# Counting four token tiles per matmul in the routing rounds with 32 thresholds

## The chip, the cores and the metric

The program runs on one core of one Trainium2 chip. The metric is device time in microseconds (us) of one execution. The engines of the core work in parallel, each through its own queue of instructions in order: PE (TensorE, matmuls; its weight loads are shown as PEld), DVE (VectorE), ACT (ScalarE), POOL (GpSimd) and SP (SyncE, which here issues DMAs).

## What is computed

Three blocks stand behind one another: a linear attention over 8 batches, 8 heads, 576 tokens and 64 channels; a mixture of experts with exact, balanced routing; a feed-forward block of width 2048. The change lies in the routing of the second:

```python
N, D = x.shape                  # 4608, 512
E = w_gate.shape[1]             # 8 experts
cap = N // E                    # 576 tokens for each
flat = (x @ w_gate).flatten()
for idx in np.argsort(-flat):
    tok, e = (int(idx) // E, int(idx) % E)
    if assigned[tok] >= 0 or counts[e] >= cap:
        continue
    assigned[tok] = e
    counts[e] += 1
...
out[mask] = np.maximum(x[mask] @ w1[e], 0.0) @ w2[e]
```

So the token-expert pairs are taken from the largest logit down, and an expert that has its 576 tokens is closed.

## The kernel before, in words

**The routing** goes in 8 phases, `route(ph)` for `ph` 0 to 7. Each phase finds the expert that fills up next and the list of its 576 tokens. It looks at every token's best logit among the experts still open and searches the value at which the first expert has 576 tokens above it. The search reads the logit as a number of 31 bits and settles some bits at a time in six rounds; `ROUNDS` (line 539) gives shift and number of thresholds: two rounds with 64 thresholds, then four with 32. The last phase needs no search, so seven phases have rounds: 42 in all, 28 of them with 32 thresholds.

The 4608 tokens lie as 36 tiles (`NJ`) of 128 partitions. One round (`round`, lines 845 to 899) is a chain that goes to and fro between DVE and PE:

- `cmp` (line 860, DVE) compares every token with all thresholds: `cm`, 128 partitions by 36 tiles by thresholds, ones and zeros in bf16.
- `count` (line 872, PE) multiplies `cm` (stationary operand) with `C` (moving operand, 8 columns for each tile, a one at the token's best expert) and sums over tiles in a PSUM bank `c4`. It steps by two tiles: 18 products, each with 16 moving columns (the experts of tiles j and j+1). With 32 thresholds the stationary operand is four tiles wide all the same, 128 columns; the rows of the third and fourth tile are computed and not used. The last step (j = 34) has only two tiles left, 64 columns; it is put ahead of j = 32, so that the sum's last product is again 128 wide.
- `flags` (lines 877 and 878, DVE): of `c4` only two blocks mean something, rows of the first tile against its experts and rows of the second against its own. One instruction takes the second block negated into `odd`, one compares first block minus 576 with `odd`.
- `bcast` (line 883, PE) and `accum` (lines 887 and 890, DVE) turn the flags into the settled digit and the tokens' next digits, from which the next round's `cmp` starts.

After the rounds the phase picks the expert, ranks its tokens and makes the list `ix` (line 818), which gates the gathers of that expert's tokens (`xg`, line 956, POOL queue) and of its weights (`wst`, line 928, POOL queue).

**What runs beside it.** Phase 0 runs while attention ends. Phases 1 to 7 run inside the expert stage: for each expert, 16 steps of 12 matmuls into `hp` (line 998) and, two steps later, 12 into `yp` (line 1017); ACT and DVE make `hh` from `hp` in two parts (lines 1005 and 1009). DVE and ACT also split each expert's gathered weights into two halves (`unit`, lines 909 and 915), transpose results into `xT` (lines 973 and 977, after PE's transposes `tp`, line 967), and convert the weights of the third block (`convert_w`, lines 1099 to 1204), which SP stores to DRAM (`wdi`, line 1215) and loads again (line 1271). The units are 24 buffers that expert weights, converted weights and loads share.

**What sets the order.** A planner (`Sched`, lines 45 to 149) writes the whole stage out by hand: every step is entered with an engine, an assumed cost, what it reads and writes and a priority, and the planner issues, again and again, the step that could start first by these costs. The order on every queue comes from this plan; on the chip each engine takes its queue in order. Expert products are taken in their sequence and have the routing ahead of them (`p = -1000 + 26.51 * ph`, line 636). One plan covers the routing's phases 1 to 7 and nearly the whole expert stage; attention with phase 0 has a plan before it, and the end of the last expert and the third block have plans after it.

Of the kernel before, what the change touches and what calls it, by code (L numbers as in the profile page):

```python
# [14 lines left out]
OP = mybir.AluOpType  # L15
# [6 lines left out]
E, F, FF = 8, 1024, 2048  # L22
CAP = NT // E
NJ = NT // 128
# [587 lines left out]
class Moe:  # L612
# [17 lines left out]
    def route(self, ph, bank):  # L630
# [7 lines left out]
        def dve(cost, fn, r=(), w=(), early=False, slack=0.0):  # L638
            sc.op("DVE", cost, fn, r=[(x, ph) if isinstance(x, str) else x for x in r],
                  w=[(x, ph) if isinstance(x, str) else x for x in w], prio=0 if early else p, slack=slack, port=early)  # L640

        def pe(cost, fn, r=(), w=(), new=()):
            sc.op("PE", cost, fn, r=[(x, ph) for x in r], w=[(x, ph) for x in w], prio=p,
                  new=[("rt" if ph else "mT", (x, ph)) for x in new], slack=SLACK if ph else 0.0)
# [127 lines left out]
        def onehot(g0, g1):  # L772
            if g0 == 0:
                T["A"] = sm.tile([128, NG, 64, 2], BF, name="A", tag="cm")
            sh = [128, g1 - g0, 64, 2]
            V.tensor_tensor(T["A"][:, g0:g1], two(T["qr"][:, 0])[:, g0:g1, None, :].to_broadcast(sh),
                            c["i64"][:, None, :, :].to_broadcast(sh), op=OP.is_equal)
# [9 lines left out]
        dve(0.9, pay, r=["qr"], w=["P"])  # L787
        CH = [(0, 9), (9, 18)] if ph == 0 else [(0, 18)]
        for g0, g1 in CH:
            dve(0.0 + 0.0705 * (g1 - g0), lambda g0=g0, g1=g1: onehot(g0, g1), r=["qr"], w=["A%d" % g0] + (["A"] if g0 == 0 else []))  # L790

        def lists(g0, g1):
            if g0 == 0:
                T["ls"] = bank()
            for g in range(g0, g1):
                nc.tensor.matmul(T["ls"][:, 0:4 * NQ], T["A"][:, g].rearrange("p r j -> p (r j)"),
                                 T["P"][:, g].rearrange("p a q j -> p (a q j)"),
                                 start=(g == 0), stop=(g == NG - 1))
        for g0, g1 in CH:
            pe(0.027 * (g1 - g0), lambda g0=g0, g1=g1: lists(g0, g1), r=["A", "A%d" % g0, "P"], w=["ls"],  # L800
# [44 lines left out]
    def round(self, ph, T, n, dve, pe, bank, cuts, allw, allv):  # L845
        nc, c, sm = self.nc, self.c, self.sm
        V = nc.vector
        sh, NT_ = ROUNDS[n]
        lone = len(cuts) > 2
        first = lone and n == 0  # L850
        CH = list(zip(cuts, cuts[1:])) if first else ((0, 24), (24, NJ)) if lone and NT_ > 32 else ((0, NJ),)

        def cmp(j0, j1):
            if j0 == 0:
                T["cm"] = sm.tile([128, NJ // 2, 64, 2], BF, name="cm").rearrange("p g t j -> p (g t j)")[:, 0:NJ * NT_].rearrange(
                    "p (j t) -> p j t", t=NT_)
            if n == 0:
                T["x"] = T["x0"]
            s = [128, j1 - j0, NT_ // 2, 2]
            V.tensor_tensor(T["cm"][:, j0:j1].rearrange("p j (h i) -> p j h i", i=2), T["x"][:, j0:j1, None, :].to_broadcast(s),  # L860
                            c[f"tab{n}"].rearrange("p (h i) -> p h i", i=2)[:, None, :, :].to_broadcast(s), op=OP.is_ge)

        def count(j0, j1):

            if j0 == 0:
                T["c4"] = bank()
            js = list(range(j0, j1, 2))
            if NT_ < 64:
                js[-2:] = js[:-3:-1]
            for j in js:  # L870
                w = min(128 // NT_, j1 - j)
                nc.tensor.matmul(T["c4"][0:w * NT_, 0:2 * E], T["cm"][:, j:j + w].rearrange("p j t -> p (j t)"),  # L872
                                 self.C[:, j:j + 2].rearrange("p j e -> p (j e)"), start=(j == 0), stop=(j1 == NJ and j == js[-1]))

        def flags():
            odd = sm.tile([64, E], F32, name="odd")[0:NT_]
            V.tensor_scalar(odd, T["c4"][NT_:2 * NT_, E:2 * E], -1.0, None, op0=OP.mult)
            V.scalar_tensor_tensor(self.flags[NT_][0:NT_], T["c4"][0:NT_, 0:E], float(CAP), odd, op0=OP.subtract, op1=OP.is_ge)

        def bcast():  # L880
            t = T["nb"] = bank()
            T["nb"] = t[:, 0:E]
            nc.tensor.matmul(t[:, 0:E], c["step"][:, n:n + 1].to_broadcast([128, 128]), self.flags[NT_], start=True, stop=True)

        def accum():
            ns = T["ns"] = sm.tile([128, 1], F32, name="ns", bufs=4)
            V.tensor_reduce(ns, T["nb"], axis=AX, op=OP.max)
            if n + 1 < NR:
                x = sm.tile([128, NJ, 2], BF, name="x", bufs=2)
                V.scalar_tensor_tensor(x, T["x"], ns, T["w"][:, n + 1, :, None].to_broadcast([128, NJ, 2]), op0=OP.subtract, op1=OP.add)  # L890
                T["x"] = x
        c4, nb, fl = f"c4{n}", f"nb{n}", f"fl{n}"
        for j0, j1 in CH:
            dve(0.07 + 0.00052 * NT_ * (j1 - j0), lambda j0=j0, j1=j1: cmp(j0, j1), r=["w%d" % j0, "cm"][:2 if j0 else 1] if first else allw + ["cm"] * (j0 > 0) + ["acc"] * (n > 0) + [("ls", ph - 1)] * (n == 0 and ph > 0),
                w=["cm%d" % j0] + ["cm"] * (j0 == 0), early=first and j1 < NJ)
            pe(0.0135 * (j1 - j0), lambda j0=j0, j1=j1: count(j0, j1), r=["cm%d" % j0] + allv, w=[c4], new=[c4] if j0 == 0 else [])
        dve(0.28, flags, r=[c4], w=[fl])
        pe(0.06, bcast, r=[fl], w=[nb], new=[nb])
        dve(0.4 if n + 1 < NR else 0.1, accum, r=[nb] + allw, w=["acc"])

# [756 lines left out]
```

## Time and profile before

| what | value |
|---|---|
| time, median of 3 runs (lowest, highest) | 1421.38 us (1420.37, 1422.38) |
| the profiled execution's own time | 1418.27 us |
| its span, first to last instruction | 1416.5 us |
| mean granted TensorE clock over the span | 0.983 of full speed |
| attention and routing phase 0 | about 0 to 178 us |
| expert stage with routing phases 1 to 7 | about 178 to 645 us |
| feed-forward block | about 645 to 1416 us |

The profile shows one execution. Busy times are per engine, idle time stands in brackets with what ended it, and a matmul's length holds its run through the array: matmuls overlap, so what a group of them takes of PE is read from its start to the start of what comes next.

### The profile page before, as it was taken

What the parts mean: (1) busy time and instruction counts of PE and PEld (TensorE: products, weight loads), DVE (VectorE), ACT (ScalarE), POOL (GpSimd) and SP (SyncE); (2) the same over time, 40 slices, a digit from 0 to 9 for tenths busy, and PEclk for the clock granted to TensorE, in tenths of its full rate; (3) what the DMA queues carried; (4) which work ended last, traced back from release to release, by engine and by line L of the source; (5) the groups of instructions that cost most, each with busy time, mean ns of one, the idle gap of its engine ahead of it and who ended that gap; (6) DMA issues with size and microseconds to landing.
All of it is one profiled execution on the core that took longest, in us unless ns stands there. A gap on an engine that the chain in (4) does not pass through costs nothing.

```text
span 1416.5 us, 26771 instructions
## 1 busy us (share of the span) xinstructions
PE 1336.9 (94%) x10256; PEld 1236.3 (87%) x10256; DVE 1047.9 (74%) x2207; ACT 789.9 (56%) x1513; POOL 275.8 (19%) x314
## 2 busy tenths in 40 slices
PE   4888399999999999998999999999999999999997
PEld 4777299989999899998998989989899999999996
DVE  7797778889878767736777776877767676776664
ACT  4675125334434545535766765767667676675663
POOL 8897322332223121000001010100101000010101
PEclk9999599999999999999999999999999999999999
DMA  9997424535745979757966575766667556765640
GB/s 264 258 265 284 129 83 143 172 118 181 221 126 167 321 231 319 206 186 270 348 207 195 179 231 171 231 208 186 202 199 248 171 188 194 229 206 172 201 164 30
DMA packets 161919, 286.98 MB, mean 203 GB/s; under 512 B 25600, under 2 KB 101376, under 8 KB 161792
## 3 DMA queue, kind: packets, MB, share of 16 engines
q1 hardware_dynamic: 137680, 222.35, 51.5%
q0 software_dynamic: 15040, 52.44, 11.3%
q10 hardware_dynamic: 9072, 10.49, 2.1%
q8 instruction: 81, 1.33, 0.4%
q14 instruction: 46, 0.38, 0.1%
HBM read 235.95 MB, written 49.28 MB: 201 GB/s over the span
## 4 chain that ended last, share of the span: by engine, by line
PE 56%; issue 28%; DMA 5%; DVE 4%; POOL 3%; SPq 2%; ACT 2%; ACTq 0%; POOLq 0%; DVEq 0%
PE hp L998 14%; PE yp L1017 13%; PE yp L1483 12%; PE hp L1357 11%; PE rt L872 2%; POOL out_dram L1495 2%; DMA kh<-in_k_dram 1%; DMA wdi<-unit 1%; PE tp L967 1%; DMA q<-in_q_dram 1%; PE xp L433 1%; SPq L212 1%; DMA xg<-xd,ix 1%; DMA v<-in_v_dram 1%; DVE cm L860 0%
## 5 line engine op out<-in xcount | busy, mean ns | idle before, releaser
L1483 PE MATMUL yp<-unit,g 128*128 128x512 f32 x1728 | 431.4, 392 | 0.1
L1483 PEld LDWEIGHTS yp<-unit,g 128*128 128x128 f32 x1728 | 310.0, 188 | 56.2 <-DVE g L1395 1.0
L1357 PEld LDWEIGHTS hp<-yTa,unit 128*128 128x128 f32 x2256 | 288.4, 188 | 18.5 <-DVE hp L1446 2.9
L1357 PE MATMUL hp<-yTa,unit 128*128 128x256 f32 x2256 | 294.1, 280 | 4.1 <-DVE hp L1446 2.7
L998 PE MATMUL hp<-xT,unit 128*128 128x288 f32 x1536 | 283.0, 303 | 0.2 <-DVE hh L1009 0.2
L1017 PE MATMUL yp<-hh,unit 128*128 128x288 f32 x1500 | 265.7, 297 | 0.0
L998 PEld LDWEIGHTS hp<-xT,unit 128*128 128x128 f32 x1536 | 228.5, 190 | 1.0 <-DVE hh L1009 0.4
L1017 PEld LDWEIGHTS yp<-hh,unit 128*128 128x128 f32 x1500 | 221.1, 189 | 0.3 <-ACT ys L1024 0.2
L1495 POOL DMA_INDIRECT out_dram<-os,gix x36 | 38.1, 1059 | 799.6 <-ACT os L1491 455.1
L1005 ACT ACTIVATE hh<-hp 128x288 fp32r<-128x288 f32 x125 | 51.2, 409 | 216.0 <-PE hp L998 191.0
L1365 ACT ACTIVATE u<-hp 128x512 f32<-128x512 f32 x144 | 86.0, 597 | 117.7 <-PE hp L1357 112.3
L1382 DVE SCALAR_TENSOR_TENSOR u<-w,r 128x512 f32<-128x512 f32 x144 | 98.7, 687 | 45.4 <-ACT r L1379 44.8
L1392 ACT ACTIVATE g<-w 128x512 fp32r<-128x512 f32 x144 | 90.3, 628 | 74.5 <-DVE w L1388 73.6
L928 POOL DMA_INDIRECT wst<-in_moe_w_dram,wi x64 | 67.1, 1048 | 246.7 <-DVE unit L915 62.3
L1009 DVE SCALAR_TENSOR_TENSOR hh<-hp,hh 128x288 fp32r<-128x288 f32 x125 | 57.0, 456 | 76.4 <-ACT hh L1005 75.7
L909 ACT ACTIVATE unit<-wst 128x512 fp32r<-128x512 f32 x128 | 77.9, 646 | 48.4 <-DMA wst<-in_moe_w_dram,wi 30.5
L1395 DVE TENSOR_TENSOR g<-w,g 128x512 fp32r<-128x512 f32 x144 | 98.8, 686 | 5.6 <-ACT g L1392 4.1
L1388 DVE SCALAR_TENSOR_TENSOR w<-r,hp 128x512 f32<-128x512 f32 x144 | 98.3, 684 | 5.5
L1357 PEld LDWEIGHTS hp<-yTb,unit 128*128 128x128 f32 x768 | 99.2, 191 | 3.6
L1357 PE MATMUL hp<-yTb,unit 128*128 128x256 f32 x768 | 102.1, 283 | 0.0
L1385 DVE SCALAR_TENSOR_TENSOR r<-u,r 128x512 f32<-128x512 f32 x144 | 98.8, 687 | 1.9
L1368 DVE TENSOR_SCALAR u<-u 128x512 f32<-128x512 f32 x144 | 61.0, 425 | 50.9 <-ACT u L1365 50.4
(205 smaller groups left out, 1711.9 us busy)
## 6 DMA issues: line engine op xcount, KB each, us to landing
unit<-wdi SPq DMA_DIRECT2D x216, 512.0 KB, 4.2
unit<-wdi SPq DMA_DIRECT2D x72, 256.0 KB, 3.6
wdi<-unit SPq DMA_DIRECT2D x56, 256.0 KB, 5.3
yd<-ys ACTq DMA_DIRECT2D x15, 576.0 KB, 4.3
k<-in_k_dram SPq DMA_DIRECT2D x16, 512.0 KB, 6.5
q<-in_q_dram SPq DMA_DIRECT2D x16, 512.0 KB, 7.5
v<-in_v_dram SPq DMA_DIRECT2D x32, 256.0 KB, 6.8
xd<-xs SPq DMA_DIRECT2D x16, 512.0 KB, 6.3
```

The lines of the kernel that those rows point to most:

```text
L909: nc.scalar.activation(f, v, AF.Copy)
L928: nc.gpsimd.indirect_dma_start(out=t, out_offset=None, in_=rows, in_offset=bass.IndirectOffsetOnAxis(ap=T["wi", ph][:, g:g + 1], axis=0))
L998: MM(t, u[:, a, 128 * (f % 4):128 * (f % 4) + 128], x[:, b, k, HALF * hf:HALF * hf + HALF], start=(k == 0 and n == 0), stop=(k == 3 and n ...
L1017: MM(T["yp", ph, hf][d], u[:, a, 128 * d:128 * d + 128], t[:, b], start=(f == 0 and n == 0), stop=(f == 7 and n == 2))
L1357: MM(dst, u[:, h, a, kk], y[:, b, kk], start=first, stop=False, skip_group_check=True)
L1365: nc.scalar.activation(t, T[zp], AF.Exp)
L1382: V.scalar_tensor_tensor(T[u], T[w], 1.0, T[rk], op0=OP.add, op1=OP.mult)
L1385: V.scalar_tensor_tensor(T[rk], T[u], 2.0, T[rk], op0=OP.subtract, op1=OP.mult)
L1388: V.scalar_tensor_tensor(T[w], T[rk], 0.5, T[zp], op0=OP.add, op1=OP.mult)
L1392: nc.scalar.activation(t[:, 0], T[w], AF.Copy)
L1395: V.tensor_tensor(T[g][:, 1], T[w], T[g][:, 0].bitcast(F32), op=OP.subtract)
L1483: MM(T["op", c, t], g[:, a, 128 * t:128 * t + 128], u[:, b], start=(i == 0 and n == 0), stop=(i == 15 and n == 2))
```

## The change

For phases 1 to 6 (phase 0, which is cut into three parts, keeps the old way) and rounds with 32 thresholds, `count` steps by four tiles: nine products of 128 stationary and 32 moving columns. Four blocks of `c4` then mean something, so `flags` adds two instructions on DVE that take the third and fourth block into `odd`. The planner's costs of the two steps change with it: 0.245 us in place of 0.486 for `count`, 0.56 in place of 0.28 for `flags`.

```diff
+        four = not lone and NT_ == 32
...
             if j0 == 0:
                 T["c4"] = bank()
+            if four:
+                for j in range(0, NJ, 4):
+                    nc.tensor.matmul(T["c4"][:, 0:4 * E], T["cm"][:, j:j + 4].rearrange("p j t -> p (j t)"),
+                                     self.C[:, j:j + 4].rearrange("p j e -> p (j e)"), start=(j == 0), stop=(j == NJ - 4))
+                return
             js = list(range(j0, j1, 2))
...
             V.tensor_scalar(odd, T["c4"][NT_:2 * NT_, E:2 * E], -1.0, None, op0=OP.mult)
+            for i in (2, 3) if four else ():
+                V.scalar_tensor_tensor(odd, T["c4"][i * NT_:(i + 1) * NT_, i * E:(i + 1) * E], -1.0, odd, op0=OP.mult, op1=OP.add)
             V.scalar_tensor_tensor(self.flags[NT_][0:NT_], T["c4"][0:NT_, 0:E], float(CAP), odd, op0=OP.subtract, op1=OP.is_ge)
...
-            pe(0.0135 * (j1 - j0), lambda j0=j0, j1=j1: count(j0, j1), r=["cm%d" % j0] + allv, w=[c4], new=[c4] if j0 == 0 else [])
-        dve(0.28, flags, r=[c4], w=[fl])
+            pe((0.0068 if four else 0.0135) * (j1 - j0), lambda j0=j0, j1=j1: count(j0, j1), r=["cm%d" % j0] + allv, w=[c4], new=[c4] if j0 == 0 else [])
+        dve(0.56 if four else 0.28, flags, r=[c4], w=[fl])
```

## Rows read from the trace of the kernel before

**Rows 1.** Windows of three stages: length, each engine's busy time, PE clock, DMA share
```profile
200.00:460.00 260.00, 257.29 (x2473) 248.70 (x2473) 214.17 (x592) 99.57 (x214) 80.27 (x84) 1.00 0.51 157
460.00:645.00 185.00, 179.41 (x1339) 177.73 (x1338) 119.92 (x220) 90.68 (x191) 21.18 (x22) 0.99 0.79 253
645.00:1416.00 771.00, 759.42 (x4789) 684.95 (x4789) 555.70 (x987) 501.28 (x950) 42.40 (x71) 1.00 0.63 201
```

**Rows 2.** PE's timeline, a count with 64 thresholds: start, length, group, what follows
```profile
224.52 0.61 PE L872 MATMUL rt<-C,cm 128*128 128x16 bf16 x18
224.99 0.65 PE L998 MATMUL hp<-xT,unit 128*128 128x288 f32 x3
```

**Rows 3.** PE's timeline, counts with 32 thresholds: the first, the seventh, the last
```profile
188.69 0.80 PE L872 MATMUL rt<-C,cm 128*128 128x16 bf16 x18
189.35 1.43 PE L1017 MATMUL yp<-hh,unit 128*128 128x288 f32 x9
...
237.40 0.80 PE L872 MATMUL rt<-C,cm 128*128 128x16 bf16 x18
238.06 1.45 PE L1017 MATMUL yp<-hh,unit 128*128 128x288 f32 x9
...
420.80 0.80 PE L872 MATMUL rt<-C,cm 128*128 128x16 bf16 x18
421.46 0.65 PE L998 MATMUL hp<-xT,unit 128*128 128x288 f32 x3
```

**Rows 4.** PE's timeline from the middle of a count: its last two products
```profile
237.89 0.31 PE L872 MATMUL rt<-C,cm 128*64 128x16 bf16 x2
```

**Rows 5.** PE's timeline, the lists' products with 40 moving columns
```profile
213.47 0.63 PE L796 MATMUL rt<-P,A 128*128 128x40 bf16 x18
213.94 1.45 PE L998 MATMUL hp<-xT,unit 128*128 128x288 f32 x9
```

**Rows 6.** DVE's timeline around the flags of a round, idle time before in brackets
```profile
238.24 0.16 DVE L877 TENSOR_SCALAR odd<-rt 32x8 f32<-32x8 f32 x1 [0.53 <-PE rt L872]
238.43 0.15 DVE L878 SCALAR_TENSOR_TENSOR fl<-rt,odd 32x8 bf16<-32x8 f32 x1
238.51 0.67 DVE L977 TENSOR_TENSOR xT<-tp,xT 128x512 fp32r<-128x512 f32 x1
...
239.89 0.29 DVE L890 SCALAR_TENSOR_TENSOR x<-x,ns,w 128x72 bf16<-128x72 bf16 x1
```

**Rows 7.** DVE's waits, 200 to 460 us: us in total, times, longest
```profile
DVE hh L1009 <- ACT hh L1005: 19.9, 34, 2.1
DVE odd L877 <- PE rt L872: 8.8, 14, 1.4
DVE ns L887 <- PE rt L883: 4.3, 5, 1.1
```

**Rows 8.** PE's waits, 200 to 460 us
```profile
PE tp L967 <- DMA xg<-xd,ix: 2.3, 2, 1.4
PE tp L967 <- DVE xT L977: 0.5, 1, 0.5
```

**Rows 9.** The end of list 1 (DVE) and expert 1's first products (PE)
```profile
219.37 0.16 DVE L818 SCALAR_TENSOR_TENSOR ix<-rt,lh 128x5 int32<-128x5 f32 x1
240.22 1.83 PE L998 MATMUL hp<-xT,unit 128*128 128x288 f32 x12
```

**Rows 10.** PE's two long stalls, the ACT wait ahead of the first, the window after it
```profile
484.50 0.66 ACT L909 ACTIVATE unit<-wst 128x512 fp32r<-128x512 f32 x1 [2.09 <-DMA wdi<-unit]
487.21 0.66 PE L967 MATMUL tp<-ident,xg 128*128 128x128 f32 x4 [3.27 <-DVE xT L977]
544.25 0.66 PE L967 MATMUL tp<-ident,xg 128*128 128x128 f32 x4 [1.95 <-DVE xT L977]
488.00:492.00 4.00, 4.00 (x20) 4.00 (x20) 4.00 (x8) 2.14 (x5) 2.02 (x2) 0.57 0.92 294
```

**Rows 11.** Stores of converted weights: durations, first and last start
```profile
L1215 SPq DMA_DIRECT2D wdi<-unit x56: 359/376/1503, 313.6 to 597.6; - x56
```

## The prediction

> **What bounds the kernel now.** The windows by stage come first [rows 1]. The six phases whose rounds change lie in the expert stage; between 200 and 460 us PE is busy for 257.29 of 260 us, at full clock, and DVE for 214.17. PE sets the pace here: what is taken from its queue shortens the stage, so long as nothing else comes to stand in its place. DVE is next, with 260 - 214.2 = 45.8 us free, and that is the figure to watch, since the change adds to it. Next come the waits. PE waits 2.8 us in this stretch, for tokens gathered or for `xT`, never for the routing's `cm` [rows 8]. DVE waits 33.0 us in three groups: for `hh`, for the counts (8.8 us) and for `bcast` [rows 7]. All three hang on PE's products, so they are waits of an engine that runs ahead. Last, PE's timeline, where a group's cost is the distance from its start to the next group's start.
>
> **PE's part.** A count with 64 thresholds has 18 products and holds PE from 224.52 to 224.99, 0.47 us or 26 ns a product [rows 2]. One with 32 thresholds has 18 too, of the same 16 moving columns, and holds it from 237.40 to 238.06, 0.66 us; so do the first at 188.69 and the last at 420.80 [rows 3]. There are 6 phases x 4 = 24 of these. The 0.19 us more belong to the one product that differs, with 64 stationary columns, put next to last [rows 4]: the count's last two products start at 237.89, 0.17 us before PE is free. Nine products without such a one cost 9 x 26 ns = 0.235 us, if 32 moving columns cost no more than 16. The lists' products have 40, and 18 of them take from 213.47 to 213.94, again 0.47 us [rows 5]; so I take 26 ns. A round saves 0.66 - 0.235 = 0.425 us of PE, 24 rounds 10.2 us.
>
> The Trainium skill, TensorEngine Tiling (Array Packing), section Key Properties, says that changing the tiling mode drains the TensorE; by that rule the 0.19 us are the price of going to 64 columns and back, and go away whole, as in the sum. Were they instead spread over all products, nine would cost half of 0.66, 0.33 us, and the sum would be 24 x 0.33 = 7.9 us. Rows 2 and 3, alike but for that product, speak for the former. That lower sum is kept for the range.
>
> **DVE's part.** The two added instructions have the shape and kind of line 878's: 0.15 us, and 0.19 us from the start of one to the start of the next that needs it; what follows `fl` starts 0.08 us after it [rows 6]. So the flags take 0.19 x 3 + 0.08 = 0.65 us in place of 0.27, 0.38 more; over 24 rounds 9.1 us. The trace has no such instruction that reads partitions 64 to 127; its bounds are 0.08 us (line 878's distance to a next that does not need it) and 0.29 (line 890's length, the longest of the round's small instructions) [rows 6], 3.8 to 13.9 us in all. I take 0.19, since row 878 differs in the partitions alone; at 0.29 the chain would grow by 0.58 - 0.425 = 0.16 us a round, which the waits still cover. What hides it: the count ends 0.425 us sooner, so the round's chain stays where it was (-0.425 + 0.38), and where DVE waits for the count, as at 238.24 for 0.53 us, the wait goes and the added instructions stand in its place. Behind the flags on DVE's queue stand `xT` (238.51) and the splits of weights; they start where they did or 0.4 us later, and PE's `hh` has two steps' lead over `yp`. At nothing, then, while that cover holds: 9.1 us of work and a stage 10.2 us shorter are 19.3 of DVE's 45.8 free us. If the cover is gone, that is the first rival below.
>
> **What else moves.** The planner gets new costs, 24 x 0.24 = 5.8 us less of PE and 24 x 0.28 = 6.7 more of DVE, and so issues another order from phase 1 on, on SP's and POOL's queues also: gathers, weight loads, stores of `wdi`. None is added or removed. Its errors shrink on PE (0.486 assumed, 0.66 taken; now 0.245 and 0.235) and grow on DVE (0.28 and 0.27; now 0.56 and 0.65), 2 us over 24 rounds; small beside the 0.5 us waits that take up such slips.
>
> One place is tight. Expert 1's list ends at 219.37 and its first products start at 240.22 [rows 9], while its third part of `xT` begins at 238.51 and takes 0.67 us [rows 6], ending at 239.18: a margin of 1.0 us. Seven changed counts lie ahead of it, from 188.69 to 237.40 [rows 3], 3.0 us of PE, while the list's own chain gains next to nothing. If `xT` stood still PE would lose 2.0 us there; it stands behind a count's flags on DVE, though, and moves with them in part. I take half, 1.0 us, and keep 0 and 2.0. Later lists end long before their experts.
>
> After 460 us PE waits in two places for transposes, 3.27 and 1.95 us [rows 10]. The first has a chain that shows its kind: ACT waited for a `wdi` store to give back a unit buffer, `hh` and `xT` stood behind. It also dropped PE's granted clock to 0.57 for 4 us, 1.7 us more: a stall of 5.0 us in all. These go through as they are in the sum; stores end at 597.6 [rows 11], 47 us ahead of the stage's end, so the conversion has room to be moved by ten.
>
> **The sum.** -10.2 + 1.0 = -9.2 us. The profiled execution took 1418.27 us and would take 1409.1; it lies 3.1 us under the median of the runs, 1421.38, to which the forecast is given: **1412.2 us**.
>
> **Rivals.**
>
> *DVE becomes the bound (slower).* The routing's chain leads through DVE, and it is 82% busy between 200 and 460 us [rows 1]. If DVE's waits do not shrink, because ACT's part of `hh` and not PE ends them, all its added work lengthens the stage: 9.1 us and no gain, 1430.5 us. It decides from the point where less than 19.3 us of DVE's free time can be used; the waits for counts alone (8.8 us) fall short, so at least 10 us must come from those for `hh` (19.9 us) and from gaps. For it: 34 waits on ACT, and an in-order queue. Against: PE itself waits only 2.8 us, so ACT and DVE are not late now. The Trainium skill names the same danger on the page cited above, section PSUM Bottleneck: after TensorE is sped up, copying out of PSUM may become the bottleneck.
>
> *The gain is given back behind 460 us.* The new order may put PE's transposes behind unit buffers that a store still holds, in more places than now. Each costs 2.0 to 5.0 us by rows 10; one more gives 1414 to 1417, two 1416 to 1422. For it: DMA is at 0.79 of its share from 460 to 645 us, and PE asks for its transposes sooner. Against: the stage behind 460 is left with the same work and DVE has 65 us free there. The mirror case is that the two present stalls vanish: 3.3 + 1.7 + 2.0 = 7.0 us less at most, 1405 to 1409.
>
> *The counts cost more than said.* With half of 0.66 us for nine products: -7.9 + 1.0, 1414.5 us.
>
> **Chances.** Forecast as worked out, 1409 to 1415: 0.56. Costlier products: 0.07. Present stalls vanish: 0.08. Given back in part or whole: 0.20, half of it still under 1418.5. DVE bound: 0.09. A measurement of this kernel tells some 0.2% or 2.8 us from no change, so faster means under 1418.5: 0.56 + 0.07 + 0.08 + 0.10 = 0.81; within: 0.08; slower: 0.02 + 0.09 = 0.11. The range 1407 to 1420.5 leaves out most of the slower case, the worst part of the given-back one and the end of the lucky one, about 0.18.
>
> **What would show it.** Right: counts of nine products with 0.23 to 0.25 us to the next group's start, no 128*64 form in them outside phase 0, three instructions 0.19 us apart and then `fl`, waits for counts below 8.8 us, PE still over 98% busy between 200 and 450, the third block starting some 9 us sooner. Wrong: waits of PE at lines 872 or 883 for DVE, DVE at over 92% there, list 1 later than 219.4, or transposes that wait for 3 us or more in new places after 450 us with the clock down behind them.

## The result and the profile after

The changed kernel took **1401.61 us** (median of five runs, 1399.23 to 1403.55), the kernel before 1421.38 (five runs, 1416.96 to 1422.38): a ratio of 0.9868, 95% interval 0.9851 to 0.9885. It is faster by 19.8 us, where 9.2 were forecast, and lies below the range. Its profiled execution took 1401.61 us, with a span of 1399.8.

Lines of the changed kernel: the four-tile `count` is 872, the old one 880; `flags` are 885, 887 (the two added instructions) and 888; `bcast` is 893; `hp`, `yp`, `tp`, `xT`, `hh`, `xg`, `wst` are 1008, 1027, 977, 987, 1019, 966, 938.

The profile after, windows of the first two stages of [rows 1] (length, busy time of PE, of its weight loads, of DVE, ACT and POOL, PE's clock, DMA share, GB/s):

```profile
200.00:460.00 260.00, 258.32 (x2354) 251.15 (x2353) 227.44 (x649) 106.75 (x229) 85.48 (x86) 1.00 0.55 173
460.00:645.00 185.00, 179.09 (x1355) 176.98 (x1353) 118.87 (x219) 92.22 (x194) 20.18 (x20) 1.00 0.78 256
```

PE is as full as it was between 200 and 460 us, and DVE has 13.3 us more work in the same stretch.

PE's timeline after, three counts with what follows each, for [rows 3]:

```profile
186.86 0.39 PE L872 MATMUL rt<-C,cm 128*128 128x32 bf16 x9
187.10 1.14 PE L1027 MATMUL yp<-hh,unit 128*128 128x288 f32 x6
...
233.37 0.39 PE L872 MATMUL rt<-C,cm 128*128 128x32 bf16 x9
233.61 0.65 PE L1027 MATMUL yp<-hh,unit 128*128 128x288 f32 x3
...
237.78 0.39 PE L872 MATMUL rt<-C,cm 128*128 128x32 bf16 x9
238.11 0.46 PE L977 MATMUL tp<-ident,xg 64*128 64x64 f32 x4
```

From start to next start a count now takes 0.24 us in 21 of 24 places; in the three that are followed by a transpose with 64 rows it takes 0.32 or 0.33.

DVE's timeline after, the flags of one round, for [rows 6]:

```profile
225.74 0.16 DVE L885 TENSOR_SCALAR odd<-rt 32x8 f32<-32x8 f32 x1 [0.35 <-PE rt L872]
225.94 0.36 DVE L887 SCALAR_TENSOR_TENSOR odd<-rt,odd 32x8 f32<-32x8 f32 x2
226.33 0.15 DVE L888 SCALAR_TENSOR_TENSOR fl<-rt,odd 32x8 bf16<-32x8 f32 x1
226.41 0.67 DVE L987 TENSOR_TENSOR xT<-tp,xT 128x512 fp32r<-128x512 f32 x1
```

The chain takes 0.67 us, 0.20 + 0.39 + 0.08. DVE's waits and PE's waits after, 200 to 460 us (us in total, times, longest), for [rows 7, 8]:

```profile
DVE hh L1019 <- ACT hh L1015: 18.0, 28, 2.2
DVE odd L885 <- PE rt L872: 0.8, 2, 0.4
DVE odd L885 <- PE rt L880: 0.8, 2, 0.5
DVE ns L897 <- PE rt L893: 0.3, 1, 0.3
```

```profile
PE rt L872 <- DVE cm L863: 1.2, 1, 1.2
PE rt L893 <- DVE fl L888: 0.5, 1, 0.5
```

DVE hardly waits for counts any more (1.6 us, 8.8 before), and PE's waits for gathered tokens (2.3 us before) are gone. Behind 460 us PE still stands twice for transposes, in other lengths, for [rows 10]:

```profile
472.07 0.66 PE L977 MATMUL tp<-ident,xg 128*128 128x128 f32 x4 [1.48 <-DVE xT L987]
...
527.33 0.66 PE L977 MATMUL tp<-ident,xg 128*128 128x128 f32 x4 [1.69 <-DVE xT L987]
```

**Where the time went.** Both traces hold a stretch with the same work: from the stage's 25th `hp` product, the first that waits for `hh`, to the second 512-column product of line 1424 (1434 after). Windows over just this stretch, before and after:

```profile
183.15:645.41 462.26, 453.55 (x3986) 442.56 (x3987) 347.29 (x842) 196.29 (x417) 103.17 (x108) 1.00 0.61 193
```

```profile
181.31:628.41 447.10, 441.48 (x3770) 431.94 (x3770) 352.02 (x890) 196.10 (x416) 108.32 (x109) 1.00 0.62 199
```

It is 15.2 us shorter. PE's idle time fell from 8.7 to 5.6 us. The clock cost 1.7 us before, 4 us at 0.57 [rows 10], and nothing after (worked out from windows of 4 us: length times what the clock lacks). What is left of PE's busy time fell by 453.55 - 1.7 - 441.48 = 10.4 us. So 15.2 = 10.4 of work + 3.1 of idle time + 1.7 of clock. Another 1.8 us lies ahead of the stretch and 0.3 the other way behind it; together the 16.7 us between the spans. The 1.8 are not the change's: that start fell anywhere between 179.7 and 184.5 us in the experiments, and at 179.7, 181.3 and 184.2 in three profiles of the changed kernel itself. The last 3.1 us of the 19.8 are the distance of before's profiled execution from its median.

### The profile page after: what moved, and what is told of

It is laid out like the page before. It is cut to its first block, busy times and chain, and to the rows that moved or that the text cites. A ratio compares the mean times of both kernels' runs of the same rounds, so it can differ in the third digit from the quotient of the medians.

```text
span 1399.8 us, 26356 instructions
## 1 busy us (share of the span) xinstructions
PE 1327.4 (95%) x10040; PEld 1229.3 (88%) x10040; DVE 1052.5 (75%) x2255; ACT 790.4 (56%) x1513; POOL 281.3 (20%) x314
## 4 chain that ended last, share of the span: by engine, by line
PE 56%; issue 28%; DVE 6%; DMA 4%; POOL 2%; SPq 2%; ACT 1%; ACTq 0%; POOLq 0%; DVEq 0%
PE hp L1008 13%; PE yp L1027 13%; PE yp L1493 13%; PE hp L1367 12%; POOL out_dram L1505 2%; DMA kh<-in_k_dram 1%; DMA wdi<-unit 1%; PE xp L433 1%; PE tp L977 1%; SPq L212 1%; PE rt L880 1%; DVE cm L863 1%; DMA w<-in_moe_w_out_dram 1%; DVE km L248 1%; DMA q<-in_q_dram 0%
## 5 line engine op out<-in xcount | busy, mean ns | idle before, releaser
L1008 PE MATMUL hp<-xT,unit 128*128 128x288 f32 x1536 | 277.6, 299 | 0.5 <-DVE hh L1019 0.5
L1008 PEld LDWEIGHTS hp<-xT,unit 128*128 128x128 f32 x1536 | 225.4, 188 | 1.3 <-DVE hh L1019 0.7
```

The lines of the kernel that those rows point to most:

```text
L1008: MM(t, u[:, a, 128 * (f % 4):128 * (f % 4) + 128], x[:, b, k, HALF * hf:HALF * hf + HALF], start=(k == 0 and n == 0), stop=(k == 3 and n ...
```

## The experiments

They ran on four chips, B to E, each beside the kernel before on the same chip; the chip of the result above, which is not known, is called A. The stretch's columns are of each run's one profile, cut as above: length, PE's busy time, its idle time, and the loss by the clock. The kernel before was profiled on A and D alone, so what is set against its stretch from B, C or E goes across chips.

| run | chip | us (before there) | ratio, 95% | length | busy | idle | clock |
|---|---|---|---|---|---|---|---|
| before | A | 1421.38 | | 462.3 | 453.6 | 8.7 | 1.7 |
| after | A | 1401.61 | 0.9868 (0.9851 to 0.9885) | 447.1 | 441.5 | 5.6 | 0 |
| e1_old_plan | B | 1412.07 (1418.89) | 0.9948 (0.993 to 0.9966) | 455.7 | 445.2 | 10.4 | 1.7 |
| e2_new_plan | B | 1411.49 (1418.89) | 0.9952 (0.9934 to 0.997) | 456.2 | 451.0 | 5.2 | 0 |
| e3_17_wide | B | 1407.19 (1418.89) | 0.9923 (0.9909 to 0.9937) | 453.1 | 447.6 | 5.5 | 1.7 |
| e4_flags_double | B | 1406.11 (1418.89) | 0.9912 (0.9898 to 0.9927) | 447.6 | 442.8 | 4.8 | 0 |
| e5_flags_065 | C | 1424.04 (1426.21) | 0.9993 (0.998 to 1.0006) | 467.8 | 449.9 | 17.8 | 6.8 |
| e6_count_cost_only | C | 1421.73 (1426.21) | 0.9964 (0.9947 to 0.9982) | 469.1 | 451.3 | 17.7 | 8.5 |
| e7_flags_cost_only | C | 1425.08 (1426.21) | 0.9991 (0.9978 to 1.0005) | 471.8 | 449.7 | 22.2 | 8.5 |
| e8_gather_behind | C | 1419.64 (1426.21) | 0.9957 (0.994 to 0.9974) | 461.6 | 447.1 | 14.5 | 3.4 |
| r_before | D | 1431.25 (1431.59) | 1.0001 (0.9985 to 1.0016) | 475.3 | 459.4 | 15.9 | 8.5 |
| r_after | D | 1419.83 (1431.59) | 0.9918 (0.9898 to 0.9938) | 461.7 | 447.9 | 13.9 | 5.1 |
| r_flags_065 | D | 1427.11 (1431.59) | 0.9969 (0.9951 to 0.9987) | 472.5 | 449.4 | 23.0 | 6.8 |
| r_flags_cost_only | D | 1427.44 (1431.59) | 0.9981 (0.9962 to 1.0) | 469.1 | 449.2 | 19.9 | 6.8 |
| q_after | E | 1404.02 (1420.11) | 0.9878 (0.9858 to 0.9898) | 447.9 | 442.9 | 5.0 | 1.7 |
| q_old_plan | E | 1413.46 (1420.11) | 0.9957 (0.994 to 0.9974) | 456.1 | 444.5 | 11.6 | 0 |
| q_new_plan | E | 1411.92 (1420.11) | 0.9943 (0.9923 to 0.9962) | 455.5 | 451.1 | 4.4 | 0 |
| q_gather_behind | E | 1418.7 (1420.11) | 0.9981 (0.9967 to 0.9996) | 464.9 | 449.7 | 15.2 | 8.5 |

**The change in its two halves.** The change has two halves that can be had one without the other: other instructions (nine products, four blocks), and other costs for the planner, that is, another order on every queue. e1_old_plan takes the new instructions with the costs of before, so that all queues keep before's order; e2_new_plan takes the instructions of before with the new costs, so that all queues have after's order. The traces bear this out: by the tiles that are named, every engine's queue has the same sequence in e1_old_plan as in before, and in e2_new_plan as in after.

```diff
 (e1_old_plan, against after)
-            pe((0.0068 if four else 0.0135) * (j1 - j0), ...
-        dve(0.56 if four else 0.28, flags, r=[c4], w=[fl])
+            pe(0.0135 * (j1 - j0), ...
+        dve(0.28, flags, r=[c4], w=[fl])
 (e2_new_plan, against after)
-            if four:
-                for j in range(0, NJ, 4):
...
-            for i in (2, 3) if four else ():
-                V.scalar_tensor_tensor(odd, ...
```

> The changed kernel (nine products, four blocks in the flags) with the planner's old costs, 0.486 and 0.28 us, so that every queue keeps the order of the kernel before. Theory A, two sources that add up: the products give 10.2 us, the new order gives the rest of the 19.8 us through fewer stalls of PE. Then this run is 9 to 11 us under the kernel before, 1410 to 1412 us, and PE still waits some 3.3 and 2.0 us for transposes behind 460 us. Theory B, the shorter counts themselves remove the stalls and the order is nothing: it is as fast as the changed kernel, 1400 to 1404 us. Theory C, the order does most: the gain is under 6 us.

> The kernel before (18 products, two blocks) with the planner's new costs, 0.245 and 0.56 us, so that every queue has the order of the changed kernel. Theory A: faster than before by what the order is worth, 5 to 9 us, 1412 to 1417 us, with waits for transposes of about 1.5 us as in the changed kernel. Theory B: as before, 1419 to 1423 us. Theory C: 12 us or more faster.

Each half alone gave about the same, 6.8 us and 7.4 us. With before's order the nine products brought PE's busy time down by 8.4 us, and 1.7 of that went to longer idle time. With after's order the old products needed their full time, but PE had no wait at all between 200 and 460 us. Both ran again beside the changed kernel on chip E:

> Nine products in the old order. As before: 0.993 to 0.997 of the kernel before, PE's work 8 to 10 us less and its idle time up.

> 18 products in the new order. As before: 0.993 to 0.997, PE's work within 1 us of the kernel before and its idle time 3 us or more down.

> The changed kernel beside its two halves on one chip. If the halves add up, it lies as far under the kernel before as the next two together, 0.987 to 0.992 of it.

The halves gave 6.7 and 8.2 us, 14.9 together, and the whole 16.1: within their intervals they add up. Windows from 200 to 460 us on chip E, of q_old_plan, of q_new_plan and of q_after:

```profile
200.00:460.00 260.00, 254.72 (x2318) 245.32 (x2317) 224.60 (x643) 102.74 (x221) 81.38 (x85) 1.00 0.52 162
```

```profile
200.00:460.00 260.00, 260.00 (x2490) 252.29 (x2487) 216.61 (x598) 103.48 (x222) 83.83 (x85) 1.00 0.52 162
```

```profile
200.00:460.00 260.00, 259.97 (x2375) 252.87 (x2374) 229.03 (x652) 106.81 (x230) 85.42 (x86) 1.00 0.54 172
```

PE is full in both kernels that have the new order and idle for 5.3 us in the one that has the old. PE's stalls there, from the timeline of q_old_plan:

```profile
306.17 0.55 PE L977 MATMUL tp<-ident,xg 128*128 128x128 f32 x3 [0.85 <-DMA xg<-xd,ix]
...
312.91 0.52 PE L977 MATMUL tp<-ident,xg 128*128 128x128 f32 x3 [0.81 <-DMA xg<-xd,ix]
...
371.40 0.44 PE L977 MATMUL tp<-ident,xg 128*128 128x128 f32 x2 [2.10 <-DVE xT L987]
```

The third stood at 0.46 us in the kernel before (at 373.82): with a faster PE and the same order, 1.6 us of the products' gain turn into waiting for a transpose's copy.

Sorted by group, from each start to the next with waits and clock taken off, the stretch's counts take 9.8 to 10.1 us less with nine products in either order. The `hp` and `yp` products, the same 3012 in every kernel, take 411.5 us in before, 412.9 and 413.8 in e1_old_plan and q_old_plan, and 410.3 to 410.8 in after and its three relatives of the new order (e2_new_plan, q_new_plan, q_after). So in the old order 1.4 to 2.3 us of what the counts save come back in products that did not change.

**The product with 64 columns.** e3_17_wide is the changed kernel with 17 products in a count, all 128 stationary columns wide; the result is the same.

```diff
-                for j in range(0, NJ, 4):
+                for j in [NJ - 4] + list(range(0, NJ - 4, 2)):
+                    m = 4 if j == NJ - 4 else 2
```

> The changed kernel with 17 products in place of nine, all with 128 stationary columns (tiles 32 to 35 in one product with 32 moving columns, the others in steps of two tiles with 16); result and order are those of the changed kernel. If the product with 64 columns alone made the difference between 0.66 and 0.47 us, a count holds PE for 17 x 26 ns = 0.44 us, and the run is 24 x (0.44 - 0.235) = 4.9 us slower than the changed kernel, 1406 to 1407 us. If the 0.19 us belong to counts with 32 thresholds as such, a count takes 0.62 us and the run is 9 us slower, 1410 to 1411 us.

PE's timeline of e3_17_wide, a count and what follows:

```profile
186.27 0.59 PE L873 MATMUL rt<-C,cm 128*128 128x32 bf16 x17
186.72 1.43 PE L1028 MATMUL yp<-hh,unit 128*128 128x288 f32 x9
```

17 products of one width take 0.45 us, 18 with one of 64 columns among them 0.66 [rows 3]. The narrow product cost the 0.19 us, and not the number of products. PE's work in the stretch is 447.6 - 1.7 = 445.9 us, 4.4 more than after's 441.5 on another chip, against the 4.9 expected.

**DVE's cover.** e4_flags_double puts two more instructions into each of the 24 flags; they add the blocks times zero.

```diff
+            for i in (2, 3) if four else ():
+                V.scalar_tensor_tensor(odd, ..., 0.0, odd, op0=OP.mult, op1=OP.add)
```

> The changed kernel with two more instructions in each of the 24 flags, which add the third and fourth block once more, times zero: 9.1 us more of VectorE's work in the chain of the rounds, order as in the changed kernel. If VectorE's part is covered, as forecast, the time stays within 3 us of the changed kernel, 1400 to 1405 us, and PE's waits in the rounds stay under 5 us. If it is at its limit already, the 9.1 us show for the most part, 1408 to 1411 us.

The median was 1406.11 us, 1 us above what was expected with the added work covered and 2 below what was expected without cover; the profiled execution, the fastest of the five, took 1401.58. Its waits of DVE, 200 to 460 us, first line, and all its waits of PE there:

```profile
DVE hh L1021 <- ACT hh L1017: 12.4, 22, 1.8
```

```profile
PE tp L979 <- DVE xT L989: 0.8, 3, 0.4
```

In this profile DVE's waits for `hh` shrank by 5.6 us more, and PE waited 0.8 us: there, doubling the added work reached PE hardly at all. The median leaves it open. It lies 4.5 us above after's on chip A, up to half of the 9.1 us added, and the changed kernel itself did not run on B; its ratio, 0.9912, lies above the 0.9868 and 0.9878 of the changed kernel on A and E.

**Is the order the costs' doing, or luck?** Three kernels have the changed kernel's instructions and other planner costs: e5_flags_065 with the flags at 0.65 us, nearer to the 0.67 that they take; e6_count_cost_only with only the count's cost new; e7_flags_cost_only with only the flags'.

```diff
 (e5_flags_065, and r_flags_065)
-        dve(0.56 if four else 0.28, flags, r=[c4], w=[fl])
+        dve(0.65 if four else 0.28, flags, r=[c4], w=[fl])
 (e6_count_cost_only)
-        dve(0.56 if four else 0.28, flags, r=[c4], w=[fl])
+        dve(0.28, flags, r=[c4], w=[fl])
 (e7_flags_cost_only, and r_flags_cost_only)
-            pe((0.0068 if four else 0.0135) * (j1 - j0), ...
+            pe(0.0135 * (j1 - j0), ...
```

> The changed kernel with one planner cost set as measured, flags 0.65 us in place of 0.56; instructions the same, order different. If the order is a throw of dice of some microseconds, the time lies anywhere from 1398 to 1410 us, PE's work in the expert stage stays within 2 us of the changed kernel and the difference is all in PE's idle time and clock. If better costs make better plans, it is under 1401 us.

> The changed kernel with the planner's new cost for the count alone (0.245 us), flags at the old 0.28. Same question: order as dice gives 1398 to 1412 us with PE's work unchanged within 2 us. If the new order gains because the planner now leaves VectorE more room in the flags, this one should have the stalls of the old plan and come out near it, 1409 to 1412 us.

> The changed kernel with the planner's new cost for the flags alone (0.56 us), the count at the old 0.486. If room for VectorE is what makes the new order better, it comes out near the changed kernel, 1400 to 1404 us; as dice, 1398 to 1412 us.

Their ratios, 0.9964 to 0.9993, show little or no gain. What the changed kernel gains on chip C was not measured. PE's waits, 200 to 460 us, the first line of each of the three:

```profile
PE rt L893 <- DVE fl L888: 8.5, 4, 4.6
```

```profile
PE rt L893 <- DVE fl L888: 12.0, 8, 5.0
```

```profile
PE rt L893 <- DVE fl L888: 10.8, 4, 4.6
```

Here PE stands at `bcast` for DVE's flags. DVE's own timeline in e5_flags_065 shows that DVE was not busy ahead of the longest of them, which moreover stands in a round with 64 thresholds, one that the change leaves alone:

```profile
358.44 0.68 DVE L1203 TENSOR_TENSOR unit<-cv,unit 128x512 fp32r<-128x512 f32 x1
364.12 0.17 DVE L885 TENSOR_SCALAR odd<-rt 64x8 f32<-64x8 f32 x1 [4.99 <-remote]
```

Since the kernel before was slower on chip C than on A too, it, the changed kernel and two of the three ran side by side on chip D:

> The kernel before once more, for a profile beside the next ones on the same chip. The profiles so far come from more than one chip, and the last four kernels ran where the kernel before itself took 1426 us, not 1419 to 1421. If that chip adds stalls of its own, they are in this profile if it runs there, and are not if it runs elsewhere.

> The changed kernel once more, on the same chip as the next two. If the order alone made the difference, it is again 1.2 to 1.4% under the kernel before, and ahead of the two next by 0.8% or more. If its lead came from the chip on which it ran, all three lie together.

> The changed kernel with the planner's cost of the flags at 0.65 us, once more. Order as dice: about 0.999 of the kernel before, as measured, against 0.987 for the changed kernel. Chip: 0.985 to 0.99, with the stalls of 4 to 5 us in the rounds gone.

> The changed kernel with the planner's new cost for the flags alone, once more. Order as dice: about 0.999 of the kernel before; chip: 0.985 to 0.99.

On one chip, then, the same instructions give 0.9918, 0.9969 and 0.9981 by the order alone, with intervals that leave the first apart from the others. The cost closer to the measured one did not give the better order. How e6_count_cost_only compares stays open, since it did not run beside the changed kernel. The whole change is worth 11.8 us on D, against 19.8 on A and 16.1 on E. The waits at `bcast` do not tell these orders apart: the changed kernel has them on D as well, as its waits from 200 to 460 us show.

```profile
PE rt L893 <- DVE fl L888: 6.3, 3, 4.7
```

Nor is such idle time the change's: the kernel before had it on this chip too (DVE, then PE):

```profile
321.08 0.16 DVE L877 TENSOR_SCALAR odd<-rt 32x8 f32<-32x8 f32 x1 [5.16 <-remote]
...
321.49 0.19 PE L883 MATMUL rt<-fl,step 128*128 128x8 bf16 x1 [3.52 <-remote]
```

**One gather on POOL's queue.** In the old order a weight gather stands ahead of list 3's copies and token gathers. POOL's timeline before, and after:

```profile
300.03 1.11 POOL L928 DMA_INDIRECT wst<-in_moe_w_dram,wi  x1 [14.15 <-DVE ix L818]
301.19 0.23 POOL L826 COPY gix<-ix 64x5 int32<-64x5 int32 x1
304.63 0.65 POOL L827 COPY gix<-ix 64x4 int32<-64x4 int32 x1 [3.21 <-DMA wst<-in_moe_w_dram,wi]
305.55 1.23 POOL L956 DMA_INDIRECT xg<-xd,ix  x1 [0.27 <-POOL gix L827]
```

```profile
293.82 0.51 POOL L826 COPY gix<-ix 64x5 int32<-64x5 int32 x1 [22.21 <-DVE ix L818]
294.38 0.55 POOL L827 COPY gix<-ix 64x4 int32<-64x4 int32 x1
295.20 2.13 POOL L966 DMA_INDIRECT xg<-xd,ix  x1 [0.27 <-POOL gix L827]
```

In the new order nothing stands between list 3 and its gathers, which start 10 us sooner; 6.1 of these come from the list itself, which ends at 293.68 in place of 299.74. e8_gather_behind is e1_old_plan with that one gather put behind the token gathers, and nothing else moved.

```diff
+            if (which, ph, g) == ("w2", 2, 3) and not late:
+                T["put off"] = lambda: weight(which, g, rows, True)
+                return
...
+            if (ph, t) == (3, 4):
+                T["put off"]()
```

> The old planner costs with nine products, and one single step moved: the last weight gather of expert 2 is issued behind the gathers of list 3's tokens on POOL's queue, not ahead of them; all other queues keep their order. If this gather, which waited for a weight buffer until 300 us, is what made the tokens of expert 3 late, both waits of PE for them (0.8 and 1.4 us in the kernel before, 1.0 and 1.0 with nine products) go, the token gathers begin about 1.5 us after list 3 in place of 5.8, and the time falls by about 2 us against the old plan with nine products (some 1410 us against 1412). If the waits come from the transfers themselves, they stay.

> Nine products in the old order with the one weight gather put behind list 3's tokens. If that gather made the tokens late, 2 us under the old order with nine products, 0.0015 in the ratio, and no waits of PE for those tokens. If not, the same time.

The two token waits went, as expected, and the time did not follow: on chip E it was 5.2 us slower than q_old_plan beside it. In the place of 1.7 us of token waits there stood one wait of 6.3 us (4.8 in e8_gather_behind), in PE's timeline of q_gather_behind:

```profile
315.23 1.09 PE L982 MATMUL tp<-ident,xg 128*128 128x128 f32 x4 [6.33 <-issue]
```

So that gather alone does not explain what the new order is worth. Whether the move brought the long wait about is not shown.

## Why the prediction was wrong

**PE's part was right.** 24 counts went from 0.66 to 0.24 us, where 0.235 was said, 10.2 us forecast and 10.4 found in the stretch's work (the counts by themselves: 24 x 0.66 - 21 x 0.24 - 3 x 0.32 = 9.8; the three dearer ones stand ahead of transposes with 64 rows). Rows 2 and 3 had been read rightly: the 0.19 us belonged to the one product of another width, and the costlier alternative, 0.33 us a count, is out. By the Trainium skill, TensorEngine Tiling (Array Packing), section Key Properties, changing the tiling mode drains TensorE; the trace of e3_17_wide agrees, with 0.45 us for 17 products of one width; it does not tell a drain from another cost of the narrow product.

**DVE's part was right.** Each added instruction took 0.195 us, the chain 0.67 us where 0.65 was said. The work went where it was to go: waits for counts fell from 8.8 us to 1.6, those for `hh` from 19.9 to 18.0. The rival in which DVE becomes the bound did not come here; by the profile of e4_flags_double the cover would hold twice the addition, by its median that is open.

**Expert 1's start was not lost.** A loss of 1.0 us was put in the sum, since PE would come sooner and list 1 would not. The list's last step began at 215.86 in the trace after, 3.5 us sooner than in [rows 9], 1.8 of it from the earlier start; its third part of `xT` began at 234.58 and expert 1's products at 235.72. The margin went from 1.0 to 0.5 us and PE did not wait. That is 1.0 us of the miss. "Later lists end long before their experts" was not right for list 3: it ended at 299.74, and PE's 2.3 us of waits for tokens [rows 8], at 309.18 and 316.93, were for its gathers. They are gone in the new order.

**The step that failed** is in "What else moves": the new order was noted, its planner's errors were called small, and the stalls were put into the sum with "These go through as they are". The order was priced at nothing, and it is worth 7.4 and 8.2 us by itself (e2_new_plan, q_new_plan), close to what the products bring. In the profiles of chip A it shows as 3.1 us of idle time and 1.7 of clock, 4.8 of the miss. The clock's part is not firmly the order's: q_after has the new order and lost 1.7 us, q_old_plan has the old and lost none. What sets the orders apart in all profiles of A, B and E bar q_gather_behind is the stretch from 200 to 460 us, where PE is idle for 2.7 to 5.6 us in the old order and for 0 to 1.7 in the new; the stalls behind it differ less, 4.0 to 5.2 us at the two transposes in the old order and 2.8 to 4.7 in the new. So the waits that the sum kept "as they are" were not only the two behind 460 us. The prediction did name the two stalls behind 460 us and a case in which they vanish, at 0.08, but apart from that took the order as a source of losses. That it fell well was luck: on chip D the same instructions in two other orders left 4.5 and 4.2 us of the whole gain. The rest of the 10.6 us between forecast and median is not of the kernel: 1.8 us ahead of the stage, and the 3.1 us that were added because before's profiled execution lay under its median. After's profiled execution lay on its median.

**The rivals in other orders.** A gain given back in part is what q_old_plan shows, ahead of 460 us and not behind it: 2.1 us at a transpose at 371.40, where before had 0.46, while the stall of [rows 10] stayed (3.0 us, 3.3 before); 6.7 us are left of 10. PE waiting for DVE at `bcast`, the prediction's sign of a bound DVE, is what e5, e6 and e7 show, 8.5 to 12.0 us, but DVE itself did nothing for 4.2 to 4.3 us of the longest wait in each (4.6, 5.0 and 4.6 us), and r_before and r_after stand at `bcast` too. So DVE as the bound came true in none of these runs. From the rows of before one could have seen that the order would be dealt anew; which way it would fall could not be read from them. The range should have been open on the lower side by what the present waits and the clock were worth: 2.8 us in rounds, 5.2 behind them, 1.7 of clock.

**Left open.** In the old order the nine products lowered PE's work by 7.3 to 8.3 us only, in the new one by 9.5 to 9.9. The counts save 9.8 to 10.1 us in both, and most of the difference stands in `hp` and `yp`; why these are dearer in the old order was not found. Nor was it shown which of the many moved steps makes the new order better; one was tried, and it was not that one.

None of the kernels run had a lower ratio than the changed one, and none points to a kernel that would.

## What to carry to other kernels

Where an order is written out by a planner, a change of an operation's cost is two changes: price the operation from the trace, and test the new order with the old instructions and the old order with the new ones before either is given the credit. A matmul of another tile width inside a run of equal ones is worth taking out where it costs what it did here, 0.19 us in 0.66: its price is the distance between two counts that differ in it alone. When a trace shows waits that a new order can touch, the range has to be open towards their vanishing as well as towards new ones.

## What the runs showed of the hardware

The price of changing the tile showed in a second place: a count of nine takes 0.24 us ahead of a 128-row product and 0.32 or 0.33 ahead of a transpose of 64 rows, 0.08 us more.

The stage can hold stretches in which PE, DVE and ACT stand still together. Counting those over 0.6 us, all eight profiles on chips C and D have some, 2.4 to 12.6 us in sum, whatever the order (6.5 in r_before, 6.0 in r_after); of the ten on A, B and E only q_gather_behind has, 3.9 us. In q_gather_behind, where PE's wait of 6.3 us was put down to "issue", the windows read:

```profile
309.00:311.00 2.00, 0.00 (x0) 0.00 (x0) 0.00 (x0) 0.00 (x0) 0.04 (x1) 1.00 0.95 357
315.50:318.00 2.50, 2.50 (x20) 2.35 (x18) 1.38 (x4) 0.93 (x3) 0.32 (x1) 0.50 0.40 121
```

The DMA engines are full at 0.95 while PE, DVE and ACT do nothing and POOL next to nothing, and when PE begins again its granted clock is 0.50, the lower of its two levels, so that this stop is paid for a second time. The same kernel before took 1418.89 to 1431.59 us by chip, and its stretch held 8.7 us of idle time on one and 15.9 on another. Why everything waits there is not shown by these traces; it is left open. Two profiles of one kernel from two chips should not be compared in this stage without a third of the kernel before beside them.
